# Two block-diagonal products as pairs of 64x64 matmuls, with more prepared sets and a third input tile

## The chip, the cores and the metric

The kernel runs on one core of a Trainium2 chip. The metric is the device time of one execution in microseconds. An execution has 32736 profiled instructions; all matrix work is float32, or float32 rounded for PE (fp32r) in the second part.

## What is computed

A delta-rule attention over 768 tokens, and a mixture of experts on its output (shapes: 4 batches, 8 heads, head size 40; 3072 tokens of 320 values, 8 experts with 1024 hidden values).

```python
for t in range(S):
    y[:, :, t] = einsum('bhd,bhde->bhe', r_t, state)
    Sa = einsum('bhde,bhe->bhd', state, a_t)
    state = state * w_t[:, :, None, :] - einsum('bhd,bhe->bhde', Sa, b_t) + einsum('bhd,bhe->bhde', v_t, k_t)
x = y.transpose(0, 2, 1, 3).reshape(B * S, H * D)
P = exp(x @ w_gate - max)
for _ in range(8):
    P /= P.sum(1) + 1e-9;  P /= P.sum(0) + 1e-9;  P *= N / E
out = sum over e of P[:, e] * (relu(x @ w1[e]) @ w2[e])
```

## The kernel before, in words

**The attention** (function `attention`) works in 12 chunks c of 64 tokens for each of 4 batches b, so 48 steps (c, b). The 8 heads lie as 4 pairs p: one head of a pair in the lower half of the partitions, the other in the upper half.

`prep(c, b)` prepares a step. It loads the input tile `inp` (line 121; two buffers in turn, the first loads use places in sets that aren't needed yet), runs two scans on DVE for the decays (q, line 128, and g in ge, line 137), multiplies kb (line 148) and ab (lines 154 and 155), forms ll on PE (line 160) and the transposes kt (line 168), and writes sx and bb. A prepared step is a *set*: sx, bb, cc and ge; there are NSX of them in turn, so the preparation of step n needs the set of step n - NSX back. In bb, used with 104 columns, the first head of a pair stands in rows 0 to 63, columns 0 to 39, the second in rows 64 to 127, columns 64 to 103; the rest is zeros that POOL writes at a set's first use (line 104). Part of ll goes to DRAM (ld).

For each group of two chunks the 64 triangular matrices of ll are loaded from there, one to a partition (lu, line 372), and inverted on DVE in blocks of 32 (lines 185 to 208 and 362); the results go to DRAM (ud, nd; lines 364 and 365). `tload(c)` (lines 241 to 248) loads them into `tt`, the tile of the matrices T of a chunk: 16 matrices of 128x128 with one head's 64x64 in each diagonal quarter and zeros elsewhere (POOL clears both tiles at the start, line 98). `tmat(c)` computes the block off the diagonal with 32x32 matmuls, gp (line 257) and op (line 263), and copies it into tt.

`recur(c, b)` is the step itself: loads rv (line 271) and f (line 273), av on PE (line 282), f on DVE (line 283), xc (line 290, two heads apart), copies x1 and c1 on ACT (lines 296 and 297), then the product with T and the one with bb that the change touches:

```python
for p in range(NP):
    nc.tensor.matmul(pu[:, p], lhsT=tts[c][:, b * NP + p], rhs=x1[:, p], ...)     # line 301
# pm = pu * mask on DVE, line 303
for p in range(NP):
    nc.tensor.matmul(c2[:, p], lhsT=pp["bb"][:, p], rhs=pm[:, p], ...)            # line 308, c in the profile
# ws = c2 + c1 on DVE, line 310
```

From ws come the output y (POOL, line 314) and the next state z (line 323), transposed (zt, line 328) into rv of the next chunk (lines 330 and 331). `gate` (lp, line 338) computes the router's values.

**The order.** `ev` lists each piece with a due time: steps at 5 c + k + 1.1 b, the preparation of step n at the time at which step n - NSX frees its set, or later by the group's own schedule (P0, PD). A scheduler orders each engine's instructions by these priorities and a timeline of its own, up to the eighth block of the MoE; every engine and SP's DMA queue then run their list in order, and an instruction that waits holds up those behind it.

**The MoE** takes 128 blocks of (expert, part, half of the tokens): seven products p in layer 1 (line 573), op in layer 2 (line 638), hl and sm on DVE. Its weights are loaded as ws (line 501) and split on ACT (lines 513 to 524) and POOL, its inputs x as xs (lines 536 and 538) and split on DVE (lines 545 to 561). The first pools of the MoE lie where the attention's inputs, the inverse's tiles and the sets that are done first lay (in the order of their last use); the rest lies where the attention's last tiles are.

Of the kernel before, what the change touches and what calls it, by code (L numbers as in the profile page):

```python
# [11 lines left out]
F32 = mybir.dt.float32  # L12
F32R = mybir.dt.float32r
AF = mybir.ActivationFunctionType
ALU = mybir.AluOpType
# [5 lines left out]
NP = 4  # L21
# [8 lines left out]
def attention(ctx, tc, d, xd, ps, pq, pt, gs, lg):  # L30
# [19 lines left out]
    for n in range(NCH * NB - NSX, NCH * NB):  # L50
        i, pool = n % NSX, sets[n - NCH * NB + NSX]
        if i in IN_SETS or i in KB_SETS:
            raw = pool.tile([128, 1512], F32, name=f"st{i}")
            raws[i] = raw
            sx_b[i] = raw[0:R2, 0:832].rearrange("r (p h x) -> r p h x", h=2, x=104)
            bb_b[i] = raw[:, 832:1248].rearrange("r (p x) -> r p x", x=104)
            cc_b[i] = raw[0:R2, 1248:1252]
            ge_b[i] = raw[0:RL, 1252:1512].rearrange("r (p t) -> r p t", t=65)
            continue
        sx_b[i] = pool.tile([R2, NP, 2, 104], F32, name=f"sx{i}")  # L60
        bb_b[i] = pool.tile([128, NP, 104], F32, name=f"bb{i}")
        cc_b[i] = pool.tile([R2, NP], F32, name=f"cc{i}")
        ge_b[i] = pool.tile([RL, NP, 65], F32, name=f"ge{i}")
    tt_b = [const.tile([128, 4 * NP, 128], F32, name=f"tt{i}") for i in range(NTB)]
    ltt = const.tile([128, 2, 4 * NP, 32], F32, name="lt2")
    lt_b = [[ltt[i * 64:i * 64 + 64, k] for k in range(2)] for i in range(2)]
    t2_b = [const.tile([128, 2 * NP, 32], F32, name=f"t2{i}") for i in range(2)]
# [49 lines left out]

    def prep(c, b, ld):
        cb = c * NB + b
        inp = raws[IN_MAP[cb]][0:RL, 0:1032] if IN_MAP.get(cb) else pin.tile([RL, 1032], F32, name="inp", bufs=2)  # L120
        nc.sync.dma_start(out=inp, in_=d["inp"][c, b, :, 0:1032])
        w65 = inp[:, 0:264]
        kb_in = inp[0:R2, 264:776].rearrange("r (p k t) -> r p k t", p=NP, k=2)
        a_in = inp[:, 776:1032].rearrange("r (p t) -> r p t", p=NP)
        qr = pin.tile([RL, NP, 65], F32, name="q")
        q = qr[:, ::-1]
        with tc.issue_after(scans[-1].ins) if cb >= N_SP else nullcontext():
            nc.vector.tensor_tensor_scan(  # L128
                out=qr.rearrange("r p t -> r (p t)"), data0=w65[:, 260:0:-1], data1=one65,
                initial=0.0, op0=ALU.mult, op1=ALU.add)  # L130
        g1 = rot("g1", g1_b)
        nc.vector.reciprocal(out=g1[:, :, 0], in_=q[:, :, 64])
        sx = rot("sx", sx_b)
        i = next(j for j in range(NSX) if sx_b[j] is sx)
        bb, cc, ge = bb_b[i], cc_b[i], ge_b[i]
        g = ge[:, :, 0:64]
        scans.append(nc.vector.tensor_tensor_scan(
            out=ge.rearrange("r p t -> r (p t)"), data0=w65[:, 0:260],
            data1=g1.rearrange("r p t -> r (p t)"), initial=0.0, op0=ALU.mult, op1=ALU.add))
        if cb < NKB:  # L140
            raw = raws[KB_SETS[cb % len(KB_SETS)]]
            kb = raw[0:R2, 0:512].rearrange("r (p k t) -> r p k t", p=NP, k=2)
            lt = raw[0:64, 512:1024].rearrange("r (p k t) -> r p k t", p=NP, k=2)
        else:
            kb = pin.tile([R2, NP, 2, 64], F32, name="kb")
            lt = pin.tile([64, NP, 2, 64], F32, name="lt")
        eng = nc.vector if cb < NFAST else nc.gpsimd
        (nc.gpsimd if cb in KB_POOL else eng).tensor_tensor(
            out=kb, in0=kb_in,
            in1=q[0:R2, :, 63::-1].unsqueeze(2).broadcast_to([R2, NP, 2, 64]), op=ALU.mult)  # L150
        ab = rot("ab", ab_b)
        first_use(i)
        nc.gpsimd.tensor_copy(out=cc, in_=q[0:R2, :, 64])
        eng.tensor_tensor(out=ab[0:40, :, 0:64], in0=a_in[0:40], in1=g[0:40], op=ALU.mult)  # L154
        eng.tensor_tensor(out=ab[64:104, :, 64:128], in0=a_in[64:104], in1=g[64:104], op=ALU.mult)  # L155
        nc.scalar.copy(out=sx[64:104, :, 0, 0:64], in_=ab[0:40, :, 0:64])
        nc.scalar.copy(out=sx[64:104, :, 1, 0:64], in_=ab[64:104, :, 64:128])
        ll = pq.tile([128, NP, 2, 64], F32, name="ll", tag="pq")
        for p in range(NP):
            nc.tensor.matmul(ll[:, p], lhsT=kb[:, p], rhs=ab[:, p], start=True, stop=True)  # L160
        if cb < NKB:
            nc.scalar.activation(out=lt, in_=ll[64:128], func=AF.Copy, scale=-1.0)
            (nc.sync if cb < N_SP else nc.scalar).dma_start(out=ld[GRP[c][1], :, b], in_=lt)
            kt = pt.tile([128, NP, 2, 64], F32, name="kt", tag="pt")
        else:
            kt = pq.tile([128, NP, 2, 64], F32, name="kt", tag="pq")
        for p in range(NP):
            nc.tensor.transpose(kt[:, p].rearrange("s h x -> s (h x)")[:, 0:R2],
                                kb[:, p].rearrange("r k s -> r (k s)"), ident[0:R2, 0:R2])
        nc.vector.tensor_tensor(  # L170
            out=sx[0:64, :, :, 0:64], in0=ll[0:64],
            in1=mask_u.unsqueeze(1).unsqueeze(1).broadcast_to([64, NP, 2, 64]), op=ALU.mult)
        if cb >= NKB:
            nc.scalar.activation(out=lt, in_=ll[64:128], func=AF.Copy, scale=-1.0)
        nc.scalar.copy(out=sx[0:64, :, :, 64:104], in_=kt[0:64, :, :, 0:40])
        nc.scalar.activation(out=bb[0:64, :, 0:40], in_=kt[64:128, :, 0, 0:40], func=AF.Copy, scale=-1.0)
        nc.scalar.activation(out=bb[64:128, :, 64:104], in_=kt[64:128, :, 1, 0:40], func=AF.Copy, scale=-1.0)
        if cb >= NKB:
            (nc.sync if cb < N_SP else nc.scalar).dma_start(out=ld[GRP[c][1], :, b], in_=lt)
        return dict(cc=cc, g=g, sx=sx, bb=bb)  # L180
# [53 lines left out]
    def tload(c):  # L234
        tt, (lb, t1), t2 = rot("tt", tt_b), rot("lt", lt_b), rot("t2", t2_b)
        tts[c], tls[c] = tt, (lb, t1, t2)
        ld, ud, nd = invs[GRP[c][0]]
        cc = GRP[c][1]
        u = [slice(cc * 64 + blk * 32, cc * 64 + blk * 32 + 32) for blk in range(2)]
        for h in range(2):  # L240
            nc.sync.dma_start(out=lb[h * 32:h * 32 + 32],
                              in_=ld[cc, 0:32].rearrange("j b p h s -> j (b p) h s")[:, :, h, 32:64])
        nc.sync.dma_start(out=t1, in_=nd[u[0]].rearrange("(g h) j s -> (h j) g s", h=2))
        nc.sync.dma_start(out=t2, in_=ud[u[1]].rearrange("(g q) j s -> (q j) g s", q=4))
        for h in range(2):
            for blk in range(2):
                r = slice(h * 64 + blk * 32, h * 64 + blk * 32 + 32)
                nc.sync.dma_start(out=tt[r, :, r], in_=ud[u[blk]].rearrange("(g h) j s -> (h j) g s", h=2)[h * 32:h * 32 + 32])  # L248

    def tmat(c):  # L250
        tt, (lb, t1, t2) = tts[c], tls[c]
        hq = [slice(q * 32, q * 32 + 32) for q in range(4)]
        with tc.high_priority(T_PRI):
            gp = pt.tile([128, 2 * NP, 32], F32, name="gp", tag="pt")
            for g in range(4 * NP):
                for h in range(2):
                    nc.tensor.matmul(gp[hq[g % 2 * 2 + h], g // 2], lhsT=lb[hq[h], g], rhs=t1[hq[h], g],
                                     start=True, stop=True)
            nc.scalar.copy(out=mt, in_=gp)
            op = pt.tile([128, 2 * NP, 32], F32, name="op", tag="pt")  # L260
            for g in range(2 * NP):
                for q in range(4):
                    nc.tensor.matmul(op[hq[q], g], lhsT=mt[hq[q], g], rhs=t2[hq[q], g], start=True, stop=True)
            for q in range(4):
                r = q % 2 * 64
                nc.scalar.copy(out=tt[r:r + 32, q // 2::2, r + 32:r + 64], in_=op[hq[q]])

    def recur(c, b):
        pp = preps[c, b]
# [28 lines left out]
        yield  # L298
        pu = ps.tile([128, NP, 104], F32, name="pu", tag="ps")
        for p in range(NP):  # L300
            nc.tensor.matmul(pu[:, p], lhsT=tts[c][:, b * NP + p], rhs=x1[:, p], start=True, stop=True)  # L301
        pm = wk.tile([128, NP, 104], F32, name="pm")
        nc.vector.tensor_tensor(out=pm, in0=pu, in1=mask_p.unsqueeze(1).broadcast_to([128, NP, 104]),
                                op=ALU.mult)
        yield
        c2 = ps.tile([R2, NP, 104], F32, name="c2", tag="ps")
        for p in range(NP):
            nc.tensor.matmul(c2[:, p], lhsT=pp["bb"][:, p], rhs=pm[:, p], start=True, stop=True)
        ws = wk.tile([R2, NP, 104], F32, name="ws")
        nc.vector.tensor_tensor(out=ws, in0=c2, in1=c1, op=ALU.add)  # L310
        if b % 2 == 0:
            ys[c, b // 2] = rot("y", y_b)
        y = ys[c, b // 2]
# [105 lines left out]
PD = 0.75  # L419
INV_DT = 0.05  # L420
SKEW = 1.1
NSX = 19
GL = 3
NFB = 3
KB_POOL = (1,2,3,4,5,6,7)
# [401 lines left out]
```

## Time and profile before

| | |
|---|---|
| runs | 1807.26, 1811.9, 1816.87 us; median 1811.9 us |
| the profiled execution's own time | 1813.25 us |
| its span, first to last instruction | 1811.3 us |
| granted TensorE clock, mean | 0.951 of full speed |
| PE busy | 1691.7 us (93%) |
| DVE, ACT, POOL busy | 1361.3, 842.0, 868.8 us |
| chain that ended last, by engine | PE 75%, DVE 11%, DMA 5%, issue 3% |

Busy time is counted from the records of instructions, and a matmul's record is longer than its turn on PE: passes that follow each other every 91 ns have records of about 255 ns. So the pace of PE is read from the starts of successive instructions, and its busy share only says where it hardly rested. The granted clock is the share of full speed that PE's clock had. A name in the profile such as c<-pm,bb is an instruction's output and inputs; st stands for sets that share a tile with early inputs. An idle time is written with the instruction that it ended before and with what ended it.

### The profile page before, as it was taken

To read this page: it belongs to the slowest core of one execution; us is meant where nothing else is said; L and a number is where in the kernel's file an instruction comes from. 1 tells how busy PE (TensorE), PEld (TensorE's weight loads), DVE (VectorE), ACT (ScalarE), POOL (GpSimd) and SP (SyncE) were. 2 spreads that over 40 slices of the span, in tenths; PEclk is the share of its full clock that TensorE was granted. 3 is DMA by queue.
4 is the path that set the end of the run, shared out by engine and by line. 5 is a ranking of instruction groups with operands and counts; after the bars stand their busy time and mean duration, and the time that the engine had idled before them with its cause. 6 is when DMAs were issued, how large, how long until landed. Compare 5 with 4: busy or idle time off the path is not lost.

```text
span 1811.3 us, 32736 instructions
## 1 busy us (share of the span) xinstructions
PE 1691.7 (93%) x12611; PEld 1668.9 (92%) x12611; DVE 1361.3 (75%) x2353; ACT 842.0 (46%) x1811; POOL 868.8 (48%) x850
## 2 busy tenths in 40 slices
PE   5468978898889999999999999999999999999999
PEld 4368878898888999999999999999999999999999
DVE  6887986974788677768686778867686777767675
ACT  6357767756534443434343444345343443434342
POOL 7555645614553453719173553009173553719160
PEclk8569989987899999999999999999999999999999
DMA  8478688577311111102010112202010111102001
GB/s 200 106 152 199 161 178 200 141 149 180 107 44 39 39 39 38 58 20 76 19 58 25 53 39 72 58 1 76 20 57 25 52 39 39 58 20 76 19 20 44
DMA packets 178737, 135.61 MB, mean 75 GB/s; under 512 B 119190, under 2 KB 160790, under 8 KB 178582
## 3 DMA queue, kind: packets, MB, share of 16 engines
q1 hardware_dynamic: 174901, 127.79, 27.1%
q10 hardware_dynamic: 3680, 5.74, 1.2%
q8 instruction: 99, 1.62, 0.4%
q14 instruction: 57, 0.46, 0.1%
HBM read 111.48 MB, written 22.02 MB: 74 GB/s over the span
## 4 chain that ended last, share of the span: by engine, by line
PE 75%; DVE 11%; DMA 5%; issue 3%; POOL 2%; SPq 2%; ACT 2%; ACTq 0%; DVEq 0%; POOLq 0%
PE op L638 36%; PE p L573 34%; DVE pr L194 1%; PE xc L290 1%; DVE q L128 1%; DMA lu<-ld 1%; PE pu L301 1%; SPq L248 1%; DMA inp<-in_inp_dram 1%; DVE un L197 1%; DMA rv<-in_rv_dram 1%; DVE sm L591 1%; DVE gt L197 1%; POOL ab L154 1%; DMA ld<-lt 1%
## 5 line engine op out<-in xcount | busy, mean ns | idle before, releaser
L573 PE MATMUL p<-xch,wh 128*128 128x384 f32 (+1 forms) x1792 | 605.9, 339 | 8.4 <-DVE sm L591 4.3
L594 ACT ACTIVATE hh<-sm 128x384 fp32r<-128x384 f32 x512 | 269.4, 527 | 729.9 <-DVE sm L591 729.9
L638 PE MATMUL op<-wh,hh 128*128 128x320 f32 x1536 | 477.2, 311 | 3.5 <-ACT hh L594 3.3
L638 PE MATMUL op<-wl,hh 128*128 128x320 f32 x1536 | 475.0, 310 | 0.0
L638 PE MATMUL op<-wh,hl 128*128 128x320 f32 x1536 | 468.9, 310 | 0.9 <-DVE hl L597 0.9
L519 POOL TENSOR_TENSOR wl<-ws,wh 128x640 fp32r<-128x640 f32 x60 | 102.8, 1714 | 608.9 <-ACT wh L517 608.7
L597 DVE SCALAR_TENSOR_TENSOR hl<-sm,hh 128x384 fp32r<-128x384 f32 x512 | 368.5, 753 | 1.9 <-ACT hh L594 1.3
L573 PEld LDWEIGHTS p<-xch,wh 128*128 128x128 f32 (+1 forms) x1792 | 337.7, 189 | 12.6 <-DVE sm L591 5.2
L573 PE MATMUL p<-xcl,wh 128*128 128x384 f32 x896 | 302.9, 338 | 0.0
L573 PE MATMUL p<-xch,wl 128*128 128x384 f32 x896 | 302.1, 337 | 0.0
L638 PEld LDWEIGHTS op<-wh,hh 128*128 128x128 f32 x1536 | 290.3, 189 | 4.4 <-ACT hh L594 4.4
L638 PEld LDWEIGHTS op<-wl,hh 128*128 128x128 f32 x1536 | 291.1, 190 | 0.0
L638 PEld LDWEIGHTS op<-wh,hl 128*128 128x128 f32 x1536 | 287.8, 188 | 1.3 <-DVE hl L597 1.2
L591 DVE TENSOR_TENSOR sm<-p,u 128x384 f32<-128x384 f32 x384 | 237.8, 629 | 8.9
L573 PEld LDWEIGHTS p<-xcl,wh 128*128 128x128 f32 x896 | 169.0, 189 | 0.0
L573 PEld LDWEIGHTS p<-xch,wl 128*128 128x128 f32 x896 | 168.9, 189 | 0.0
L591 DVE TENSOR_TENSOR sm<-p,p 128x384 f32<-128x384 f32 x128 | 71.3, 557 | 129.7 <-PE p L573 77.9
L591 DVE TENSOR_TENSOR p<-p,p 128x384 f32<-128x384 f32 x128 | 71.1, 555 | 103.5 <-PE p L573 103.1
L591 DVE TENSOR_TENSOR u<-p,p 128x384 f32<-128x384 f32 x128 | 70.8, 553 | 61.0 <-PE p L573 59.7
L527 POOL TENSOR_TENSOR wl<-ss,wh 128x512 fp32r<-128x512 f32 x60 | 90.2, 1503 | 31.5 <-ACT wh L524 27.4
L160 PE MATMUL ll<-ab,kb 104*128 104x128 f32 x336 | 62.0, 342 | 43.3 <-POOL ab L155 24.3
L160 PEld LDWEIGHTS ll<-ab,kb 104*128 104x128 f32 x336 | 53.9, 244 | 48.7 <-POOL ab L155 27.4
(164 smaller groups left out, 2642.7 us busy)
## 6 DMA issues: line engine op xcount, KB each, us to landing
ws<-in_wts_dram SPq DMA_DIRECT2D x60, 832.0 KB, 4.5
inp<-in_inp_dram SPq DMA_DIRECT2D x42, 451.5 KB, 4.7
rv<-in_rv_dram SPq DMA_DIRECT2D x48, 336.0 KB, 5.0
xd<-y SPq DMA_DIRECT2D x24, 224.0 KB, 2.9
ld<-lt ACTq DMA_DIRECT2D x40, 128.0 KB, 3.8
f<-in_vt_dram SPq DMA_DIRECT2D x48, 80.0 KB, 2.7
out_dram<-acc SPq DMA_DIRECT2D x42, 80.0 KB, 2.1
lu<-ld SPq DMA_DIRECT2D x24, 128.0 KB, 3.2
```

Of the source, the lines that this page charges most:

```text
L128: nc.vector.tensor_tensor_scan(out=qr.rearrange("r p t -> r (p t)"), data0=w65[:, 260:0:-1], data1=one65, initial=0.0, op0=ALU.mult, op1=A ...
L154: eng.tensor_tensor(out=ab[0:40, :, 0:64], in0=a_in[0:40], in1=g[0:40], op=ALU.mult)
L160: nc.tensor.matmul(ll[:, p], lhsT=kb[:, p], rhs=ab[:, p], start=True, stop=True)
L194: nc.vector.tensor_tensor(out=prv, in0=a.unsqueeze(2).broadcast_to([nu, n_c, n_r, n_k]), in1=m.unsqueeze(1).broadcast_to([nu, n_c, n_r, n_ ...
L197: nc.vector.tensor_reduce(out=dst, in_=prv, op=ALU.add, axis=AX.X)
L519: g.tensor_tensor(out=wl[:, 0:640], in0=raw[:, 256:896], in1=wh[:, 0:640], op=ALU.subtract)
L527: g.tensor_tensor(out=lv[:, 3:7], in0=so[:, :, 0], in1=hv[:, 3:7, 0], op=ALU.subtract)
L573: nc.tensor.matmul(o, lhsT=w_, rhs=x_, start=(j == 0), stop=(j == 3))
L591: eng.tensor_tensor(out=out, in0=x, in1=y, op=ALU.add)
L594: nc.scalar.activation(out=hh[:, f, h], in_=sm[f][:, h], func=AF.Relu)
L597: v.scalar_tensor_tensor(out=hl[:, f, h], in0=sm[f][:, h], scalar=0.0, in1=hh[:, f, h], op0=ALU.max, op1=ALU.subtract)
L638: nc.tensor.matmul(ops[i], lhsT=a[:, h, cs], rhs=w_[:, cw], start=(f == 0 and h == 0 and j == 0), stop=(last and h == 1 and j == 2))
```

## The change

bb has 64 columns instead of 104 (both heads in columns 0 to 39), and tt 16 matrices of 128x64, both heads' blocks in columns 0 to 63. Each product of a pair of heads becomes two matmuls of 64x64, one on partitions 0 to 63 and one on 64 to 127, each into its own half of pu or c2; c2 is 128 partitions instead of 104, and ws reads its first 104. A set takes 5408 bytes of a partition instead of 6048 and a tile of T 4096 instead of 8192. There are 22 sets instead of 19, and three buffers for `inp` instead of two.

```diff
-            raw = pool.tile([128, 1512], F32, name=f"st{i}")
+            raw = pool.tile([128, 1352], F32, name=f"st{i}")
...
-            bb_b[i] = raw[:, 832:1248].rearrange("r (p x) -> r p x", x=104)
+            bb_b[i] = raw[:, 832:1088].rearrange("r (p x) -> r p x", x=64)
...
-        bb_b[i] = pool.tile([128, NP, 104], F32, name=f"bb{i}")
+        bb_b[i] = pool.tile([128, NP, 64], F32, name=f"bb{i}")
...
-    tt_b = [const.tile([128, 4 * NP, 128], F32, name=f"tt{i}") for i in range(NTB)]
+    tt_b = [const.tile([128, 4 * NP, 64], F32, name=f"tt{i}") for i in range(NTB)]
...
-        inp = raws[...] if IN_MAP.get(cb) else pin.tile([RL, 1032], F32, name="inp", bufs=2)
+        inp = raws[...] if IN_MAP.get(cb) else pin.tile([RL, 1032], F32, name="inp", bufs=3)
...
-        nc.scalar.activation(out=bb[64:128, :, 64:104], in_=kt[64:128, :, 1, 0:40], func=AF.Copy, scale=-1.0)
+        nc.scalar.activation(out=bb[64:128, :, 0:40], in_=kt[64:128, :, 1, 0:40], func=AF.Copy, scale=-1.0)
...
-                nc.sync.dma_start(out=tt[r, :, r], in_=...)
+                nc.sync.dma_start(out=tt[r, :, blk * 32:blk * 32 + 32], in_=...)
...
-                nc.scalar.copy(out=tt[r:r + 32, q // 2::2, r + 32:r + 64], in_=op[hq[q]])
+                nc.scalar.copy(out=tt[r:r + 32, q // 2::2, 32:64], in_=op[hq[q]])
...
         for p in range(NP):
-            nc.tensor.matmul(pu[:, p], lhsT=tts[c][:, b * NP + p], rhs=x1[:, p], start=True, stop=True)
+            for o in (slice(0, 64), slice(64, 128)):
+                nc.tensor.matmul(pu[o, p], lhsT=tts[c][o, b * NP + p], rhs=x1[o, p], start=True, stop=True)
...
-        c2 = ps.tile([R2, NP, 104], F32, name="c2", tag="ps")
+        c2 = ps.tile([128, NP, 104], F32, name="c2", tag="ps")
         for p in range(NP):
-            nc.tensor.matmul(c2[:, p], lhsT=pp["bb"][:, p], rhs=pm[:, p], start=True, stop=True)
+            for o in (slice(0, 64), slice(64, 128)):
+                nc.tensor.matmul(c2[o, p], lhsT=pp["bb"][o, p], rhs=pm[o, p], start=True, stop=True)
...
-        nc.vector.tensor_tensor(out=ws, in0=c2, in1=c1, op=ALU.add)
+        nc.vector.tensor_tensor(out=ws, in0=c2[0:R2], in1=c1, op=ALU.add)
...
-NSX = 19
+NSX = 22
```

With other due times and sizes the scheduler orders nearly every list anew (two more lines in the file move the numbers behind line 301 by one or two). Three places follow.

PE early in the program, behind the first T. Before:

```order
L290 MATMUL xc_1062<-f,sx_169 104x104 x4
L290 MATMUL xc_1063<-f,sx_169 104x104 x4
L282 MATMUL av<-rv_210 104x128 x4
L328 MATMUL zt<-cst,z 40x104 x4
L308 MATMUL c_1126<-pm,bb_166 104x104 x4
L301 MATMUL pu<-x_1072,tt_198 128x104 x4
L160 MATMUL ll<-ab_205,kb 128x128 x4
L168 MATMUL kt<-cst,kb 128x104 x4
```

And with the change:

```order
L290 MATMUL xc_1096<-f,sx_211 104x104 x4
L282 MATMUL av<-rv_231 104x128 x4
L160 MATMUL ll<-ab_225,kb 128x128 x3
L168 MATMUL kt<-cst,kb 128x104 x4
L330 MATMUL zt<-cst,z 40x104 x4
L310 MATMUL c_1159<-pm,bb_208 64x104 x8
L302 MATMUL pu<-x_1105,tt_219 64x104 x8
L290 MATMUL xc_1217<-f,sx_215 104x104 x4
```

The 4 matmuls of c and of pu become 8 each, mostly still side by side. In the whole list the tile size of PE (128 rows, 64x64, 32x32) changes between small and full 162 times; before, with gp and op alone, 44 times.

DVE at the start of the program, from the first preparation's ab (lines 154 and 155). Before:

```order
L154 TENSOR_TENSOR ab_204<-st_152,ge_164 40x4x64
L155 TENSOR_TENSOR ab_204<-st_152,ge_164 40x4x64
L170 TENSOR_TENSOR sx_161<-ll,cst 64x8x64
L128 SCALAR_TENSOR_TENSOR q<-st_151,cst 112x260
L132 RECIPROCAL g_206<-q 112x4
L137 SCALAR_TENSOR_TENSOR ge_168<-st_151,g_206 112x260
```

And with the change:

```order
L154 TENSOR_TENSOR ab_225<-st_182,ge_206 40x4x64
L155 TENSOR_TENSOR ab_225<-st_182,ge_206 40x4x64
L128 SCALAR_TENSOR_TENSOR q<-st_181,cst 112x260
L132 RECIPROCAL g_227<-q 112x4
L137 SCALAR_TENSOR_TENSOR ge_210<-st_181,g_227 112x260
L170 TENSOR_TENSOR sx_203<-ll,cst 64x8x64
```

The second preparation's scans stand ahead of the first one's sx; on PE the first av stands behind the second ll, where it stood ahead of it.

SP's queue where the MoE's first loads are issued (ws are weights, xs inputs of the MoE; ud, nd, t, lt and tt belong to T). Before:

```order
L317 DMA xd<-y_215 448x1x128
L501 DMA ws<-in_wts_dram 128x1664 x2
L536 DMA xs<-xd 128x2x256
L538 DMA xs<-xd 32x2x256
L273 DMA f<-in_vt_dram 64x8x40
L538 DMA xs<-xd 32x2x256 x2
L271 DMA rv_209<-in_rv_dram 112x4x192
```

And with the change:

```order
L243 DMA lt_221<-nd 64x16x32
L503 DMA ws<-in_wts_dram 128x1664 x2
L538 DMA xs<-xd 128x2x256
L540 DMA xs<-xd 32x2x256 x2
L273 DMA f<-in_vt_dram 64x8x40
L540 DMA xs<-xd 32x2x256
L271 DMA rv_229<-in_rv_dram 112x4x192
```

The same row of loads stands earlier: 10 loads of f come behind the first ws, 4 before; it now stands ahead of the eight loads into the last two tiles of T instead of behind them. On PE, 42 of the 48 av stand ahead of the first MoE matmul, 46 before.

## Rows read from the trace of the kernel before

**Rows 1.** The page: 40 slices of the span, busy tenths and granted clock.
```profile
PE   5468978898889999999999999999999999999999
...
DVE  6887986974788677768686778867686777767675
...
PEclk8569989987899999999999999999999999999999
```

**Rows 2.** Stretches: length, busy us (instructions) of each engine, clock, DMA share, GB/s.
```profile
0.00:45.00 45.00, 23.51 (x126) 21.54 (x127) 31.34 (x60) 28.08 (x68) 31.43 (x55) 0.83 0.86 201
...
136.00:362.00 226.00, 195.22 (x2407) 187.94 (x2406) 186.12 (x328) 164.14 (x414) 135.45 (x165) 0.92 0.77 176
362.00:408.00 46.00, 42.96 (x609) 41.79 (x609) 35.98 (x64) 27.47 (x71) 9.07 (x13) 0.89 0.70 146
...
437.00:463.00 26.00, 23.64 (x127) 22.72 (x128) 21.15 (x32) 18.99 (x41) 16.25 (x16) 0.56 0.53 132
...
611.00:1811.00 1200.00, 1196.30 (x7518) 1195.05 (x7516) 882.39 (x1505) 476.92 (x939) 541.25 (x467) 1.00 0.13 42
```

**Rows 3.** Groups by line, 0 to 680 us: shapes, count, busy us, idle before.
```profile
L301 PE MATMUL pu<-x,tt 128*128 128x104 f32 x384 | 59.8, 301 | 4.3 <-ACT c L297 2.3 <-ACT tt L266 1.6 <-ACT rv L331 0.2
```

**Rows 4.** Timeline of PE, 383 to 387.9 us: start, us from it to the last end.
```profile
383.22 0.90 PE L308 MATMUL c<-pm,st 128*104 128x104 f32 x8
383.95 1.06 PE L301 MATMUL pu<-x,tt 128*128 128x104 f32 x8
384.84 0.75 PE L338 MATMUL lp<-gs,y 104*128 104x8 f32 x6
385.53 0.77 PE L263 MATMUL op<-t,mt 32*32 32x32 f32 x64
386.23 1.71 PE L290 MATMUL xc<-f,st 104*104 104x104 f32 x16
387.78 0.38 PE L282 MATMUL av<-rv 104*104 104x128 f32 x2
```

**Rows 5.** The same timeline in two narrow windows: op's neighbours, pass by pass.
```profile
385.34 0.26 PE L338 MATMUL lp<-gs,y 104*128 104x8 f32 x1
...
386.11 0.19 PE L263 MATMUL op<-t,mt 32*32 32x32 f32 x1
```

**Rows 6.** Waits of DVE, 115 to 437 us: us in total, times, longest.
```profile
DVE q L128 <- DMA inp<-in_inp_dram: 17.8, 7, 4.7
```

**Rows 7.** The chain that ended last, 225 to 310 us: start, us, what.
```profile
237.12 5.37 DMA inp<-in_inp_dram
...
278.25 4.03 DMA inp<-in_inp_dram
...
296.27 3.96 DMA inp<-in_inp_dram
```

**Rows 8.** Timelines of DVE, PE and POOL at the start of the program.
```profile
12.52 0.68 DVE L170 TENSOR_TENSOR sx<-ll,cst 64x512 f32<-64x512 f32 x1 [2.79 <-ACT st L162]
...
17.27 2.03 PE L282 MATMUL av<-rv 104*104 104x128 f32 x8 [5.42 <-DMA rv<-in_rv_dram]
...
5.64 3.56 POOL L98 MEMSET tt<- 128x2048 f32 x2
```

**Rows 9.** Around 437 us: the chain's f, then timelines of DVE and ACT.
```profile
431.07 9.19 DMA f<-in_vt_dram
...
438.95 0.69 DVE L283 TENSOR_TENSOR f<-av,cst 104x512 f32<-104x512 f32 x1 [5.88 <-PE av L282]
442.19 1.00 DVE L545 TENSOR_TENSOR xt<-xs 128x256 f32<-128x256 f32 x1 [2.54 <-DMA xs<-xd]
...
434.88 0.83 ACT L513 CAST wh<-ws 128x768 fp32r<-128x768 f32 x1 [4.13 <-DMA ws<-in_wts_dram]
```

**Rows 10.** The page: DMA issues, count, KB each, median us to landing.
```profile
ws<-in_wts_dram SPq DMA_DIRECT2D x60, 832.0 KB, 4.5
inp<-in_inp_dram SPq DMA_DIRECT2D x42, 451.5 KB, 4.7
```

More of the change, by code (lines that the diff above doesn't have):

```diff
@@ L52, in attention @@
         if i in IN_SETS or i in KB_SETS:
-            raw = pool.tile([128, 1512], F32, name=f"st{i}")
+            raw = pool.tile([128, 1352], F32, name=f"st{i}")
             raws[i] = raw
             sx_b[i] = raw[0:R2, 0:832].rearrange("r (p h x) -> r p h x", h=2, x=104)
-            bb_b[i] = raw[:, 832:1248].rearrange("r (p x) -> r p x", x=104)
-            cc_b[i] = raw[0:R2, 1248:1252]
-            ge_b[i] = raw[0:RL, 1252:1512].rearrange("r (p t) -> r p t", t=65)
+            bb_b[i] = raw[:, 832:1088].rearrange("r (p x) -> r p x", x=64)
+            cc_b[i] = raw[0:R2, 1088:1092]
+            ge_b[i] = raw[0:RL, 1092:1352].rearrange("r (p t) -> r p t", t=65)
             continue
         sx_b[i] = pool.tile([R2, NP, 2, 104], F32, name=f"sx{i}")
-        bb_b[i] = pool.tile([128, NP, 104], F32, name=f"bb{i}")
+        bb_b[i] = pool.tile([128, NP, 64], F32, name=f"bb{i}")
         cc_b[i] = pool.tile([R2, NP], F32, name=f"cc{i}")
         ge_b[i] = pool.tile([RL, NP, 65], F32, name=f"ge{i}")
-    tt_b = [const.tile([128, 4 * NP, 128], F32, name=f"tt{i}") for i in range(NTB)]
+    tt_b = [const.tile([128, 4 * NP, 64], F32, name=f"tt{i}") for i in range(NTB)]
     ltt = const.tile([128, 2, 4 * NP, 32], F32, name="lt2")
@@ L119, in prep @@
         cb = c * NB + b
-        inp = raws[IN_MAP[cb]][0:RL, 0:1032] if IN_MAP.get(cb) else pin.tile([RL, 1032], F32, name="inp", bufs=2)
+        inp = raws[IN_MAP[cb]][0:RL, 0:1032] if IN_MAP.get(cb) else pin.tile([RL, 1032], F32, name="inp", bufs=3)
         nc.sync.dma_start(out=inp, in_=d["inp"][c, b, :, 0:1032])
@@ L247, in tload @@
                 r = slice(h * 64 + blk * 32, h * 64 + blk * 32 + 32)
-                nc.sync.dma_start(out=tt[r, :, r], in_=ud[u[blk]].rearrange("(g h) j s -> (h j) g s", h=2)[h * 32:h * 32 + 32])
+                nc.sync.dma_start(out=tt[r, :, blk * 32:blk * 32 + 32], in_=ud[u[blk]].rearrange("(g h) j s -> (h j) g s", h=2)[h * 32:h * 32 + 32])
     def tmat(c):
```

## The prediction

> **What bounds the kernel now.** I read the page first. Its slices [rows 1] show two programs one behind the other: from the fourteenth on (589 us) PE is 9 tenths busy at full clock and nothing else matters; ahead of that PE, DVE and the DMA engines share the work and the clock falls twice. The change touches the first part alone, since the MoE part's instructions are the same. The stretches [rows 2] say how tight that part is. From 136 to 362 us, where chunks are prepared, inverted and stepped through together, PE is busy 195.2 of 226 us and DVE 186.1: both are near their bound and each waits for the other. From 362 to 408 us nothing is left to prepare and PE is the bound (43.0 of 46). From 437 to 463 us the attention ends while the MoE's first operands are made: PE runs 127 passes in 26 us at a granted clock of 0.56, about the 1.2 GHz level, against 609 passes in 46 us just before. At that pace 127 passes need 9.6 us, so 16 us are lost there. From 611 us on PE is busy 1196.3 of 1200 us.
>
> **Edit 1: the two products as pairs of halves.** A float32 matmul is two passes, so a step has 8 passes for pu and 8 for c (384 of pu in 48 steps) [rows 3]. Back to back, c's 8 passes take 0.73 us (383.22 to 383.95), 91 ns each, and pu's 0.89 us, 111 ns each [rows 4]; pu streams as many columns and differs in loading 128 weight columns instead of 104, so the wider load sets its pace. After the change each has 16 passes of 64x64 that stream the same 104 columns. Whether two halves run side by side isn't shown for 64x64. The nearest rows are op's: four 32x32 tiles on the array's diagonal, 64 passes in 0.70 us, from 385.53 to 386.23 [rows 4], 10.9 ns each. At c's 0.88 ns a column a lone pass of 32 columns would take 28 ns, so at least 2.6 ran at a time. I take two at a time for the pair: 8 x 91 ns = 0.73 us for either product, so pu gains 0.16 us a step and c nothing, 48 x 0.16 = 7 us less PE time. The other end is no overlap: 16 x 91 ns = 1.46 us, 0.57 us more for pu and 0.73 for c, 48 x 1.30 = 62 us more.
>
> The price is the change of tile size. Going into op, the last lp pass starts at 385.34 and the first op pass at 385.53, 0.19 us where lp passes stand 0.10 apart (384.84 to 385.34 for five): 0.09 more. Coming out, the last op pass starts at 386.11 and xc at 386.23 [rows 5], 0.12 where op's stand 0.01 apart; then xc's 16 passes take 1.55 us (to 387.78) instead of 16 x 91 ns = 1.46: 0.11 + 0.09. That is 0.29 us for a round trip. In the order of PE the tile size changes 44 times now and 162 times after, as c and pu mostly stand side by side: 59 more round trips, 59 x 0.29 = 17 us (low end 0, if 64x64 needs no such pause).
>
> PE's sum is +17 - 7 = +10 us. Not all of it is on the path: in 136 to 362 us PE has idle time of its own, in 362 to 485 us hardly. I take two thirds, **+7 us** (0 to 10).
>
> **Edit 2: the third input tile.** DVE waits for an input load 17.8 us in seven places between 115 and 437 us, up to 4.7 us each [rows 6]. The chain that ended last has three of these landings, 5.37, 4.03 and 3.96 us [rows 7]: 13.4 us in which nothing else was later. A load can start only when the tile's last reader is done, and it stands in SP's queue behind the inverse's stores and loads. With three tiles each load is issued a preparation earlier. What is late next is POOL's ab, for which PE's ll already waits, or the load of lu. I take two thirds of the chain's pieces, **-9 us** (0 to -18).
>
> **Edit 3: 22 sets, and what the order makes of them.** At the start DVE's scan for the second preparation moves ahead of the first sx, and the av that waits for rv moves behind the second ll. DVE idles 2.79 us at that sx, and PE 5.42 us ahead of av at 17.27 [rows 8]. POOL clears half as much of the tiles of T, 1.8 us less of 3.56, and fewer columns of each bb. Against that, the third input tile (451.5 KB [rows 10], 2.3 us at the 201 GB/s of [rows 2]) goes ahead of rv. **-3 us** (0 to -5). From there to 115 us the inverse of the first group runs as before, with one more preparation between its steps.
>
> Later the preparations and with them the inverses run about four steps earlier, so the MoE's first loads are issued with 10 loads of f still to come instead of 4, and 42 of the 48 av stand ahead of the first MoE matmul instead of 46. Work is not saved by that; it is the lost time of 437 to 463 us that can be filled with steps. There ACT waited 4.13 us for the weights with PE's rv copies behind it, DVE 5.88 us for av and 2.54 us for xs, and the f issued at 431.07 landed 9.19 us later, behind two weight loads of 832 KB [rows 9, 10]. In the new order the two weight loads still stand just ahead of an f and an rv, so most of this comes back at another place; more steps are in reach to cover it. I take **-6 us** of 16 (0 to -16). What waits for the end of attention (weights 2 and 3, the second half of x, the sinkhorn) lies behind it as now.
>
> The smaller DMA targets of T have the same runs of 32 values, and the copies into bb the same size: nothing.
>
> **Sum.** +7 - 9 - 3 - 6 = -11 us. The profiled execution took 1813.25 us (span 1811.3), 1.35 us above the median of the three runs, 1811.9. The forecast is **1802 us**. A measurement of this kernel can tell about 0.5%, 9 us, from no change; the forecast is just beyond that.
>
> **The rivals.**
> *DVE is the bound, PE is not.* Then PE's extra time falls into its own waits, DVE gets back all 17.8 us, the start gives its 5 and the handover its 16: 1813 - 39 = 1774 us. For it: DVE's 186 of 226 us, and its wait on inputs in the chain. Against it: PE's 86% there, and that the handover keeps its order. Chance 0.14.
>
> *Nothing is left.* The input no longer waits, but the next event is as late (PE waits for POOL's ab, DVE for lu), the handover's stall only moves, and PE's 10 us count in full: +10 - 5 - 3 - 2 gives 1813 us. For it: three engines over 80% in the middle stretch. Chance 0.23.
>
> *Slower: the halves run one after the other.* Two 64x64 tiles on different rows write one PSUM tile. If they take turns, PE has 62 + 17 = 79 us more, two thirds of it on the path, 53, less the 18 of the other edits: 1848 us. It decides from 57 ns a pass: then the 32 passes of a step take 1.83 us instead of 1.62, with the switches 27 us, and two thirds of that eat the 18. Against it: op's passes at 10.9 ns, whose four row tiles write one PSUM tile as well [rows 4]. The Trainium skill's "TensorEngine Tiling (Array Packing)", Gotcha 1: PSUM Pressure, says that different row tiles cannot access the same PSUM bank at the same time; by that rule this rival is the forecast. The rows on op disagree with it for 32x32; no row shows 64x64. Chance 0.12.
>
> *The handover gets worse.* With 10 steps still to go, an f that waits 9.19 us behind the weights stops more batches than now: instead of -6 one such wait more, +9, gives 1817 us. Chance 0.09.
>
> That the change doesn't do what it says can be excluded: its order has the 64x64 products and the earlier preparations.
>
> **How the numbers follow.** The forecast has 0.42, and its own spread from the bounds is about 1790 to 1812. Faster by over 0.5% (below 1803): 0.27 of the forecast, all 0.14 of the first rival, 0.03 of the second: 0.44. Slower by over 0.5% (above 1821): 0.12 of the halves, 0.04 of the handover, 0.04 of the second rival: 0.20. The rest, 0.36, is within. The range for 8 in 10 is 1778 to 1834: it leaves out about half of the first rival below, and most of the halves above.
>
> **What would show it.** Right: pu and c at 45 to 50 ns a pass, a run of 16 in about 0.75 us; 0.2 to 0.35 us lost on the way in and out; DVE's waits for inp well below 17.8 us, and none of 4 us in the chain; the first MoE matmul before 455 us with six steps to go; fewer than 16 us lost at the low clock around it. Wrong: passes of pu near 91 ns (the halves take turns); PE's wait for ab growing by what DVE's wait for inp shrinks (nothing is left); a longer stretch at a clock near 0.5 at the handover.

## The result, and the profile after

| kernel | median (lowest to highest), runs | against the kernel before, 95% interval |
|---|---|---|
| before, beside it | 1810.9 us, 4 | |
| the change | 1831.67 us (1826.81 to 1832.19), 4 | 1.0105 (1.0081 to 1.0129) |

The change is slower by 1.05%, about 19 us, where 11 us less was forecast. Here and below 1% is 18.1 us, and differences between runs are taken from their ratios. The profiled execution took 1832.17 us, its span 1830.4 us, at a mean clock of 0.952.

The page's slices of the change, for [rows 1]:

```profile
PE   5478888896989999999999999999999999999999
...
DVE  7885897786488767777686878977686877767676
...
PEclk8569799997989999999999999999999999999999
```

The second program looks as before from the fourteenth slice on. Its stretches, for [rows 2] (length, busy us and instructions of PE, weight loads, DVE, ACT and POOL, clock, DMA share, GB/s):

```profile
136.00:362.00 226.00, 192.30 (x2666) 174.79 (x2663) 175.44 (x313) 155.95 (x394) 128.42 (x160) 0.90 0.79 174
362.00:408.00 46.00, 42.58 (x749) 39.19 (x749) 37.36 (x65) 28.78 (x74) 10.82 (x14) 0.96 0.59 130
437.00:463.00 26.00, 19.01 (x187) 17.54 (x188) 19.31 (x30) 13.68 (x32) 15.73 (x18) 0.74 0.54 143
611.00:1811.00 1200.00, 1199.96 (x7533) 1198.92 (x7532) 883.48 (x1504) 483.56 (x954) 557.13 (x481) 1.00 0.13 42
```

In the middle stretch PE and DVE are both less busy than in [rows 2], DVE by 10.7 of 186.1 us: nothing got fuller, everybody waits more. Where the loss lies is read from the last product of the attention, the last lp on PE's timeline; first the kernel before, then the change:

```profile
487.05 0.95 PE L338 MATMUL lp<-gs,y 104*128 104x8 f32 x8
```
```profile
505.71 0.96 PE L340 MATMUL lp<-gs,y 104*128 104x8 f32 x8
```

It stands 18.7 us later, and from its end to the end of the span it is 1323.3 us before (1811.3 - 488.0) and 1323.7 after. So the whole loss is made before the attention ends. The pairs themselves do what was forecast. PE's timeline of the change, for [rows 4], and its group of pu, for [rows 3] (count, busy us, idle before):

```profile
384.16 0.93 PE L310 MATMUL c<-pm,bb 64*64 64x104 f32 x16
384.92 0.88 PE L302 MATMUL pu<-x,tt 64*64 64x104 f32 x16
385.73 1.71 PE L290 MATMUL xc<-f,st 104*104 104x104 f32 x16
387.28 1.04 PE L282 MATMUL av<-rv 104*104 104x128 f32 x8
```
```profile
L302 PE MATMUL pu<-x,tt 64*64 64x104 f32 x768 | 55.9, 279 | 3.3 <-ACT c L297 2.2 <-ACT x L296 0.4 <-ACT tt L266 0.2
```

From c's start to pu's are 0.76 us and from pu's to xc's 0.81, 48 and 51 ns for each of 16 passes: two run at a time. The xc behind them takes 1.55 us, the 0.09 us too long that it had behind op. DVE's wait for inputs, 115 to 437 us, for [rows 6], fell as forecast, from 17.8 to 3.3 us:

```profile
DVE q L128 <- POOL kb L148: 7.4, 5, 2.6
...
DVE q L128 <- DMA inp<-in_inp_dram: 3.3, 1, 3.3
```

What is new is a stall at 410 us. POOL's timeline of the change:

```profile
416.98 0.72 POOL L513 TENSOR_TENSOR ss<-ws 128x256 f32<-128x256 f32 x1 [12.23 <-DMA ws<-in_wts_dram]
...
418.34 0.72 POOL L517 TENSOR_TENSOR ss<-ss,ws 128x256 f32<-128x256 f32 x1
419.02 0.68 POOL L316 TENSOR_TENSOR y<-ws,st 104x256 f32<-104x256 f32 x1
419.65 0.45 POOL L325 TENSOR_TENSOR z<-ws,st 104x160 f32<-104x160 f32 x1
```

The MoE's ss waits for the first weights with y and z of chunk 8 behind it; until chunk 9 z is on POOL (L325), and the next step waits for z. But that can't be all. How many av passes (8 a step) PE has done by 160, 226 and 408 us, in windows of L282 that begin at 0, before and after:

```profile
0.00:160.00 160.00, 9.92 (x67) 0.72 0.70 161
0.00:226.00 226.00, 18.22 (x129) 0.77 0.72 164
...
0.00:408.00 408.00, 44.14 (x314) 0.83 0.73 165
```
```profile
0.00:160.00 160.00, 10.41 (x64) 0.72 0.74 167
0.00:226.00 226.00, 17.52 (x112) 0.74 0.71 161
...
0.00:408.00 408.00, 41.63 (x296) 0.83 0.73 163
```

At 160 us the change is nearly level, at 226 us it is 17 passes behind, and at 408 us, ahead of that stall, 18, over two steps. It has prepared as much: its scans q for the preparations number 34 by 226 us against 33 before, and 48 by 362 us in both.

### The profile page after: what moved, and what is told of

Read it like the earlier page. It is cut to its first block, busy times and chain, and to the rows that moved or that the text cites. A ratio compares the mean times of both kernels' runs of the same rounds, so it can differ in the third digit from the quotient of the medians.

```text
span 1830.4 us, 34314 instructions
## 1 busy us (share of the span) xinstructions
PE 1701.4 (93%) x13379; PEld 1659.0 (91%) x13379; DVE 1364.8 (75%) x2353; ACT 842.2 (46%) x1814; POOL 860.3 (47%) x853
## 4 chain that ended last, share of the span: by engine, by line
PE 73%; DVE 5%; issue 1%; DMA 1%; ACT 1%; SPq 0%; POOL 0%; ACTq 0%; DVEq 0%; POOLq 0%
PE op L640 36%; PE p L575 34%; PE xc L290 1%; PE c L310 1%; DVE sm L593 1%; PE pu L302 1%; DVE hl L599 1%; DVE pr L194 0%; PE av L282 0%; DVE xch L563 0%; DMA ws<-in_wts_dram 0%; PE lp L340 0%; DVE xch L558 0%; DVE u L593 0%; DVE xcl L555 0%
```

## The experiments

Each figure below is the median of 4 to 12 runs, beside runs of the kernel before on the same chip (medians 1811.1 to 1813.0 us).

### Take the change apart

Theory A was the stall at 410 us; what stood against it was that the loss lies in the pairs, spread over the steps. z8 takes z off POOL one chunk earlier:

```diff
-        (nc.vector if c >= 9 else nc.gpsimd).tensor_tensor(out=z, in0=ws[:, :, 64:104],
+        (nc.vector if c >= 8 else nc.gpsimd).tensor_tensor(out=z, in0=ws[:, :, 64:104],
```

in2 has `bufs=2` for inp again, sets19 has `NSX = 19`, and pairs_only has both: the pairs and the compact tiles alone.

> The changed kernel with one constant moved: z is computed on DVE from chunk 8 on instead of from chunk 9 on. Theory A (at the handover two z of chunk 8 stand on POOL behind a wait for the MoE's weights, and PE stands still 8.9 us for them): 8 to 12 us less than the changed kernel's 1831.7, so 1820 to 1824, and no wait of POOL's z over 3 us on PE after 400 us. Theory B (the earlier preparations have put the steps behind by 11 us before that, and the rest is the pairs' own price): within 4 us of 1831.7, since another wait at the handover ends as late. What I expect is A.

> The changed kernel with 19 sets instead of 22: pairs of halves and three input tiles stay. Theory A and B both have the loss come with 22 sets (the order they make): 1808 to 1816, about the kernel before. Theory C (the pairs and their changes of tile size cost it, 118 more changes on PE's path): 1825 to 1832, no better than the changed kernel. What I expect is about 1813.

> The change's pairs of halves alone: 19 sets and two input tiles as before. If the pairs cost what the changed kernel's rows show (c and pu with their ways in and out 1.75 us a step against 1.62 before, 48 steps, 6 us on PE): 1813 to 1818. Theory C: 1825 or more. Theory that the third input tile is worth 9 us: 9 us above the run with 19 sets and three input tiles; that it is worth nothing: equal to it within 3 us.

> The changed kernel with two input tiles instead of three: 22 sets and the pairs stay. If the third tile saves its 9 us in the changed kernel as well: 1840. If it is worth nothing there: 1828 to 1835. DVE's waits for inp between 115 and 437 us tell directly: 15 us or more with two tiles, under 5 with three.

| run | median | ratio |
|---|---|---|
| z8 | 1834.8 us | 1.0115 (1.0090 to 1.0139) |
| in2 | 1832.51 us | 1.0108 (1.0092 to 1.0124) |
| sets19 | 1844.69 us | 1.0175 (1.0157 to 1.0194) |
| pairs_only | 1847.73 us | 1.0191 (1.0174 to 1.0207) |

Theory A fell: z8 isn't faster, though its order is made anew as well, so this run alone doesn't clear the stall. Its waits from 405 to 470 us show that ss still waits as long, and that the stall has another one beside it:

```profile
POOL ss L513 <- DMA ws<-in_wts_dram: 12.3, 1, 12.3
DVE xt L547 <- DMA xs<-xd: 11.9, 1, 11.9
```

The third input tile gave nothing (in2 against the change), the sets gave 13 us, and the pairs alone cost 35 us. Theory B's time fits z8, but like A it had the loss come with the 22 sets, and with 19 the loss is larger; sets19 is slower than any of its theories had it. In in2 DVE's wait for inputs is back (115 to 437 us), and the time is the change's all the same:

```profile
DVE q L128 <- DMA inp<-in_inp_dram: 20.4, 6, 6.2
```

PE's timeline accounts for little of the 35 us: c and pu together take 1.57 us where [rows 4] have 1.62, and with their ways in and out at most 6 us more in 48 steps. The order in which the instructions stand had changed too, though, on every engine, since a scheduler makes it anew from the program. So I parted the two.

### The pairs in the old order, the old matmuls in the new one

Theory D: the order costs it. Theory C: the pairs do. The kernel is built twice. The first program is only ordered; in the second every instruction is tied behind the one that it follows in the first, an edge of order without a wait:

```diff
+def halves(lhs, rhs):
+    if not PAIRS[0]:
+        yield slice(0, lhs.shape[1]), lhs, rhs
+        return
+    for o in (slice(0, 64), slice(64, 128)):
+        yield o, lhs[o], rhs[o]
...
+    for name in final:
+        i = mirror.get(name)
...
+            e = str(j.engine)
+            if e in last:
+                tc.add_manual_dep(j, last[e].name, mybir.DependencyInfo(
+                    mybir.DependencyClass.NoSync, mybir.DependencyReason.DATA), reason="order")
+            last[e] = j
```

pairs_oldorder plans with the kernel before and runs pairs_only; full_neworder plans with pairs_only and runs the kernel before; after_ordF plans the change with one matmul for each p and runs it with pairs. All three tie the attention's instructions alone. The last line says what is planned and what is run (pairs or not, old tile sizes or not); in full_neworder it reads as below, behind the + (behind the - is pairs_oldorder's):

```diff
-PLAN, RUN, PLAN_WIDE, RUN_WIDE = False, True, True, False
+PLAN, RUN, PLAN_WIDE, RUN_WIDE = True, False, False, True
```

> The pairs and the compact tiles with 19 sets and two input tiles, but every attention instruction on every engine is held to the order in which the kernel before has it; the second matmul of a pair stands right behind the first. Theory D (the loss sits in the order that the scheduler makes of twice as many matmuls): the time of before plus PE's own price of the pairs, 1813 + 6 = 1819 us (1813 to 1825). Theory C (the loss sits in the pairs themselves, their changes of tile size and their waits): as slow as the pairs in the scheduler's own order, 1847 us (1838 to 1855).

> The kernel before with its 128-row matmuls and wide tiles, but every attention instruction is held to the order that the scheduler makes for the pairs (19 sets, two input tiles). Theory D: slow although no pair runs, about 1840 us (1833 to 1850). Theory C: like the kernel before, 1813 us (1807 to 1820).

> The changed kernel whole (pairs, 22 sets, three input tiles), but held to the order that the scheduler makes when each p of a product is one matmul, as before. Theory D: the sets give what they give and the pairs cost PE's 6 us alone, 1806 us (1798 to 1816), faster than both kernels. Theory C: no gain over the change, 1832 us (1825 to 1840).

| run | median | ratio |
|---|---|---|
| pairs_oldorder | 1825.2 us | 1.0070 (1.0057 to 1.0083) |
| full_neworder | 1835.22 us | 1.0131 (1.0116 to 1.0145) |
| after_ordF | 1798.4 us | 0.9928 (0.9914 to 0.9943) |

The order alone costs 24 us without any pair in it, and the change in the order made for single matmuls is faster than both kernels. But the pairs still cost 13 us in the old order, just more than D allows. By 408 us that run, pairs_oldorder, has the steps of before (312 av passes against 314):

```profile
0.00:408.00 408.00, 44.53 (x312) 0.84 0.72 165
```

So its loss came later. In the next run, pairs_oldorder2, the MoE's instructions are tied as well, and the tiles keep their old size (the pairs read 64 of their columns), so that order and places in memory are those of before without exception.

### What each part is worth in a good order

in2_ordF and sets19_ordF are after_ordF with `bufs=2` and with `NSX = 19`, each in the order that the scheduler makes for its own single matmuls; after_ordF2 ties the MoE's instructions too, as pairs_oldorder2 does:

```diff
-            if j is None or j.name not in attn:
+            if j is None or (j.name not in attn and str(j.engine).split(".")[1] not in ('DVE', 'Activation', 'Pool', 'SP', 'PE')):
```

> The pairs in exactly the order of before: every instruction of attention and of the MoE on all five engines, and every tile at the size that it had before (the pairs read 64 columns of the wide tiles). What is left is what the matmuls themselves do on the chip. In the run that held the attention alone to the old order 39.0 steps were done at 408 us against 39.25 before, and the 13 us were lost behind that, at the handover and in the MoE. If those 13 us came from where the MoE's instructions fell: 1812 + 1 to 7 = 1813 to 1819 us. If the pairs cost them by themselves: 1825 us (1821 to 1829).

> The run that held the change to the order made for single matmuls (1798 us), with two input tiles in place of three. If the third tile gives the 9 us of the prediction: 1807 us (1804 to 1812). If it gives nothing, as in the scheduler's own order (1832.5 against 1831.7): 1798 us (1795 to 1802).

> The same run (1798 us) with 19 sets in place of 22 and three input tiles. If the sets give the 3 us of the prediction and the order is all the rest: 1801 us (1798 to 1806). If the sets give most of what lies between 1798 us and the 1825 us of the pairs in the old order: 1812 us or more (1810 to 1825).

> The same run (1798 us), with the MoE's instructions too where the order made for single matmuls has them. If only the attention's order matters: 1798 us (1794 to 1802). If the MoE's places at the handover are worth as much as the 13 us of the pairs in the old order: 1788 us or less, or 1808 us or more.

| run | median | ratio |
|---|---|---|
| pairs_oldorder2 | 1814.79 us | 1.0017 (1.0002 to 1.0032) |
| in2_ordF | 1808.08 us | 0.9980 (0.9965 to 0.9996) |
| sets19_ordF | 1815.9 us | 1.0017 (1.0002 to 1.0032) |
| after_ordF2 | 1802.68 us | 0.9945 (0.9924 to 0.9966) |

The pairs by themselves cost 0.17%, 3 us (0.4 to 5.8); the other 10 us of pairs_oldorder came from where the MoE's instructions and tiles fell. Most of that lies behind the attention. The last lp of pairs_oldorder (span 1827.1 us), then of pairs_oldorder2 (1817.0 us):

```profile
494.55 0.95 PE L340 MATMUL lp<-gs,y 104*128 104x8 f32 x8
```
```profile
491.33 0.96 PE L340 MATMUL lp<-gs,y 104*128 104x8 f32 x8
```

From its end to the end of the span are 1331.6 and 1324.7 us, 7 of the 10 us.

The third input tile is worth 0.52%, 9 us, with 22 sets (in2_ordF against after_ordF), and the sets are worth 0.89%, 16 us, with three input tiles (sets19_ordF against after_ordF). With 19 sets, or with two tiles, the base decides. Against pairs_oldorder2 the third tile gives nothing and the sets 7 us. Against pairs_oldorder, which like these runs ties the attention alone and has the compact tiles, they give 10 and 16 us and simply add up. The 10 us between the two bases are the MoE's places, and sets19_ordF is free of that loss (1321.7 us behind its last lp). So whether the two need each other is not shown. Tying the MoE too in the good order (after_ordF2) changes nothing that the intervals can tell.

The faster run's stretches, for [rows 2], then its first MoE matmul on PE's timeline:

```profile
136.00:362.00 226.00, 198.79 (x3002) 181.98 (x3001) 190.77 (x348) 165.78 (x418) 137.46 (x162) 0.94 0.81 182
...
437.00:463.00 26.00, 23.93 (x297) 22.23 (x296) 13.90 (x24) 13.38 (x34) 10.09 (x13) 0.80 0.29 79
```
```profile
434.56 0.60 PE L575 MATMUL p<-xch,wh 128*128 128x384 f32 x2
```

Same instructions as the change, in another order: 336 more passes of PE and 35 more instructions of DVE are done in the same 226 us.

### What is wrong with the order

The second inverse shows it first. VectorE's (DVE's) list has it ahead of all but two steps in the change and in pairs_only; four steps are done by then in after_ordF and five in the kernel before. DVE's timelines, these lines alone: the ws that ends a step's work there, and the tn that ends the inverse. First the kernel before (two more ws stand ahead, at 124.00 and 130.12), then the old matmuls in the pairs' order (full_neworder2, below; one more ahead, at 124.16):

```profile
137.49 0.55 DVE L310 TENSOR_TENSOR ws<-c,c 104x416 f32<-104x416 f32 x1
...
143.64 0.57 DVE L310 TENSOR_TENSOR ws<-c,c 104x416 f32<-104x416 f32 x1
...
150.62 0.55 DVE L310 TENSOR_TENSOR ws<-c,c 104x416 f32<-104x416 f32 x1
...
151.60 0.59 DVE L362 COPY tn<-un 128x256 f32<-128x256 f32 x1
```
```profile
134.87 0.57 DVE L312 TENSOR_TENSOR ws<-c,c 104x416 f32<-104x416 f32 x1
...
141.37 0.35 DVE L364 COPY tn<-un 128x256 f32<-128x256 f32 x1
141.64 0.58 DVE L312 TENSOR_TENSOR ws<-c,c 104x416 f32<-104x416 f32 x1
...
149.98 0.56 DVE L312 TENSOR_TENSOR ws<-c,c 104x416 f32<-104x416 f32 x1
```

The inverse is done 10 us sooner, and steps wait behind it with their product ready. In the change, a c on PE and the ws on DVE that reads it:

```profile
123.73 0.93 PE L310 MATMUL c<-pm,bb 64*64 64x104 f32 x16 [0.32 <-ACT c L297]
```
```profile
130.68 0.58 DVE L312 TENSOR_TENSOR ws<-c,c 104x416 f32<-104x416 f32 x1
```

That c is done at 124.66 us, and DVE comes to its ws 6.0 us later, with four instructions of the inverse between. In the kernel before the first five ws come 1.2 to 2.5 us behind their c.

POOL, whose y and z carry a step on, waits for ws meanwhile. Its waits for it from 115 to 362 us (us in all, times, longest) in the kernel before, the change, full_neworder2 and after_ordF:

```profile
POOL y L314 <- DVE ws L310: 29.6, 17, 8.9
```
```profile
POOL y L316 <- DVE ws L312: 47.8, 14, 9.8
```
```profile
POOL y L316 <- DVE ws L312: 44.0, 17, 10.9
```
```profile
POOL y L316 <- DVE ws L312: 31.7, 14, 7.3
```

The second inverse alone can't be the loss: by 160 us, when it is done, the change is 3 av passes behind, of 18 by 408 us. I took VectorE's list as a whole for the cause, and held one engine's list at a time:

```diff
-ENGINES = ("PE", "DVE", "Activation", "Pool", "SP")
+ENGINES = ("DVE",)
```

> The changed kernel; of attention only VectorE's list is held to the order made for single matmuls, the other four are ordered by the scheduler around it. The change in its own order stands at 1831 us, with all five lists held at 1798 us. If VectorE's list carries the loss (the inverse and the preparations pulled ahead of the steps): 1803 us (1796 to 1812). If it is another list: 1825 to 1833 us.

> The changed kernel with TensorE's list alone held to the order made for single matmuls. If VectorE's list carries the loss: little changes, 1820 to 1833 us. If it is TensorE's own list (which product stands ahead of which): 1803 us (1796 to 1812).

> The changed kernel with GpSimd's list alone held. If VectorE's list carries the loss: 1820 to 1833 us. If it is where y, z and the preparations stand on GpSimd: 1803 us (1796 to 1812).

> The changed kernel with SyncE's list alone held, the DMA issues. If VectorE's list carries the loss: 1820 to 1833 us. If it is the order of the loads: 1803 us (1796 to 1812).

| run | median | ratio |
|---|---|---|
| hold_dve | 1840.96 us | 1.0167 (1.0146 to 1.0188) |
| hold_pe | 1844.22 us | 1.0187 (1.0170 to 1.0203) |
| hold_pool | 1842.17 us | 1.0176 (1.0159 to 1.0194) |
| hold_sp | 1840.58 us | 1.0162 (1.0148 to 1.0176) |

None helps; each is slower than the change with its lists free, and than either theory had it. So no one of these four lists, put right alone, takes the loss away. The inverse ahead of the steps on DVE is a sign and not the cause by itself. In hold_dve four steps are done before the second inverse, as in after_ordF, and POOL's wait for ws, 115 to 362 us, is down to that of the kernel before:

```profile
POOL y L316 <- DVE ws L312: 29.0, 13, 9.2
```

Yet hold_dve is slow: the other lists, ordered around DVE's, are not those of after_ordF. ACT's list was not held alone, nor were several held together short of all five, so which lists carry the loss stays open.

Last, from what the scheduler makes it. plan_cols4 plans the change with pairs that stream 4 columns and runs the full pairs; full_neworder2 is full_neworder with the MoE tied too.

```diff
-        yield o, lhs[o], rhs[o]
+        yield o, lhs[o], rhs[o, 0:COLS[0]]
```

> The changed kernel, with attention held to an order that the scheduler made for pairs whose matmuls stream 4 columns in place of 104: as many matmuls as in the change, nearly no work in them. The pairs that run are the full ones. If the scheduler's order is bad because it counts twice the columns for the pairs: as good as the order for single matmuls, 1800 us (1796 to 1810). If the number of matmuls is enough to make it: like the change in its own order, 1832 us (1822 to 1842).

> The kernel before with its 128-row matmuls and tiles, with every instruction, the MoE's too, in the order made for the pairs with 19 sets and two input tiles. With the pairs the same order took 1848 us. If the pairs cost as little in this order as in the old one (2 us): 1845 us (1840 to 1850). If they cost 13 us more there, as the run that held the attention alone says (1835 us): 1835 us (1830 to 1839).

| run | median | ratio |
|---|---|---|
| plan_cols4 | 1825.05 us | 1.0079 (1.0059 to 1.0099) |
| full_neworder2 | 1842.97 us | 1.0171 (1.0151 to 1.0190) |

With nearly no columns in the plan's pairs the order is nearly as bad: 1.0079, against 1.0105 planned with the full pairs and 0.9928 with single matmuls, 85% of the difference. So it is not the columns that the scheduler counts; twice the number of matmuls, and their being 64x64, are what is left, and these were not parted. And the old matmuls in the pairs' whole order take 31 us more than in their own; pairs_only, where the scheduler makes that order for the pairs, takes 35 more. In the bad order too the pairs themselves seem to cost little, about 4 us, though the two intervals overlap and the tiles' sizes differ.

The av passes by 408 us part the runs by the order alone. In orders made with pairs they are 296 (the change), 293 (z8), 296 (in2), 280 (sets19), 290 (pairs_only), 296 (full_neworder), 288 (full_neworder2) and 296 (plan_cols4). In orders made with single matmuls they are 314 (before), 312 (pairs_oldorder, pairs_oldorder2 and sets19_ordF), 327 (in2_ordF) and 328 (after_ordF, after_ordF2), whether pairs run or not. So it is not just any new order that is slow. How the scheduler comes from the pairs to these orders was not tried, nor whether other due times would mend them.

## Why the prediction was wrong

**The sum against the runs.** In the order made for single matmuls the change gives -13 us, where -11 was forecast:

| | forecast | measured |
|---|---|---|
| pairs and changes of tile size | +7 | +3 alone (pairs_oldorder2), +13 with where the MoE fell (pairs_oldorder) |
| third input tile | -9 | -9 with 22 sets, 0 or -10 with 19 |
| start and handover, from the 22 sets | -9 | -16 with three input tiles, -7 or -16 with two; not parted |
| sum, order made for single matmuls | -11 | -13 (after_ordF) |
| the order made for the pairs | 0 | +32 (1.0105 against 0.9928) |

Where the table has two numbers, the first is against pairs_oldorder2, the second against pairs_oldorder. Added in the order pairs, sets, tile, from pairs_oldorder2, the terms are near the forecast: +3, -7, -9. Added the other way, +3, 0, -16, or from pairs_oldorder, +13, -10, -16, they aren't. So the sum is confirmed and its terms are only in part; where the MoE falls, worth 10 us, was no term of it. The 1831.67 us of the change lie within the range of 1778 to 1834, but by none of the ways that were forecast or named.

**The step that failed** is a term put at nothing: what the order costs that the scheduler makes for the pairs. Edit 1 priced the pairs by PE's time alone. Edit 3 read the new order at two places, the start and the handover, put it down to the 22 sets ("Later the preparations and with them the inverses run about four steps earlier"), and let the rest stand at nothing, as if earlier preparations could only help. The runs show +32 us there, and that they come with the pairs: with 19 sets and two input tiles that order costs 24 to 31 us without any pair in the program (full_neworder, full_neworder2), while 22 sets in the order made for single matmuls gain 16 with three input tiles. The loss shows as 18 av passes that are not done by 408 us, 17 of them behind by 226. The rows of DVE and POOL above show a part of how: inverses stand in front of steps that are ready. Why the steps fall behind is open beyond that. No rival held this either; "Nothing is left" and "The handover gets worse" both kept the old pace up to 408 us.

**Edit 1** was right about the halves: 48 and 51 ns a pass with the ways in and out, where 45 to 50 were to be seen, so "the halves run one after the other" is out. The Trainium skill's "TensorEngine Tiling (Array Packing)", Gotcha 1: PSUM Pressure, says that different row tiles cannot access the same PSUM bank at the same time; these rows disagree with it, as the two halves write one PSUM tile from different rows of the array and overlap. PE's price was over-estimated by 4 us, within the bound of 0 to 10.

**Edit 2** was right about the wait, and about its worth in the good order: there DVE waits 16.9 us for inputs with two tiles (in2_ordF) and 1.2 with three (after_ordF), and 9 us are gained. In the change's own order the wait fell as forecast, from 17.8 to 3.3 us, and nothing was gained; from 115 to 437 us DVE's waits for POOL's kb grew from 0.5 to 7.4 us and those of ws for c from 8.3 to 18.0. That is "Nothing is left" in kind, but not by the wait that it named: PE's for ab fell, from 8.9 to 2.8 us.

**Edit 3.** The first MoE matmul came at 458.04 us, not before 455, with six steps to go as forecast; in the good order it came at 434.56. 437 to 463 us had 187 passes at a clock of 0.74 instead of 127 at 0.56 [rows 2], so that stretch did get better. But the two steps were missing before it, and POOL's 12.23 us behind the weights stand ahead of it as well.

## What to carry to other kernels

Where a scheduler orders the lists, an edit that splits instructions is two changes: what the chip does with the pieces, and the new order. Don't put the second at nothing; hold the old order to measure the first alone, and run the old instructions in the new order to measure the second. Here the good order was to be had: plan with the unsplit matmuls, run the split ones, 0.72% faster than the kernel before. Hold all the lists, though: with one of them alone taken from that order and the others ordered around it, the program was 10 to 15 us slower than with none (1.0162 to 1.0187 against 1.0105).

## What the runs showed of the hardware

Two 64x64 float32 matmuls, one on partitions 0 to 63 and one on 64 to 127, run at the same time though both write one PSUM tile: 16 passes of 104 columns, in turn on the two halves, take 0.76 us, 48 ns each, against 91 ns for a pass of 128x104 weights over as many columns. The change of tile size behind them made xc's 16 passes 0.09 us longer (1.55 us instead of 1.46).
